# Twelve token blocks cut as eleven of 512 and one of 384, the last of them multiplied without Strassen's scheme

## The chip, the cores and the metric

One core of a Trainium2 chip. The metric is the device time of one launch in microseconds (us); lower is better. Inputs and outputs lie in the chip's memory, and the host only lays arrays out.

## What is computed

A channel attention over 6016 tokens of 256 channels, then two feed-forward stages of width 2048, all in float32. The first stage's activation is `h * cos(h)`, the second's is `h * sigmoid(h)` (SiLU).

```python
qn = q / (np.linalg.norm(q, axis=1, keepdims=True) + 1e-06)   # q, k, v: (1, 6016, 256)
kn = k / (np.linalg.norm(k, axis=1, keepdims=True) + 1e-06)
s = kn.transpose(0, 2, 1) @ qn / tau                          # 256 x 256
a = np.exp(s - s.max(-1, keepdims=True))
a /= a.sum(-1, keepdims=True) + 1e-09
x = (v @ a).reshape(6016, 256)
h = x @ w_in;   x = (h * np.cos(h)) @ w_out                   # 256 -> 2048 -> 256
h = x @ w_in2;  out = (h * (1.0 / (1.0 + np.exp(-h)))) @ w_out2
```

The weights reach the chip as 64-bit floats (the reference draws them so) and are decoded there.

## The kernel before, in words

**Opening (L283 to L465).** The 256 x 256 scores are summed over all tokens, softmaxed, and folded into the first input weights (`emit_w`), so that the first stage reads v directly. Every product is made of three matmuls of rounded parts (fp32r): high x high, low weight x high, high weight x low (`PASSES`). So each operand is split into a high and a low tile.

**First stage (L724 to L797).** The tokens are cut into NB = 12 blocks by `SIZES` (L29): four of 512 columns and eight of 496. A block has NPAIR = 8 units, m = 0 to 7; a unit covers 256 of the 2048 hidden features. For each unit, TensorE makes h (`emit_h`, 12 matmuls of one block's width), ScalarE and VectorE make `h * cos(h)` (L495, L496, L503, L504), ScalarE and VectorE split it (L511, L512), and two units later TensorE adds it into the block's output (`emit_o1`, again 12 matmuls, L522). At a block's end its output is copied out of PSUM (L563), its Strassen forms are made and split in five steps that are popped one per unit (`emit_x2`), and the result is stored to DRAM by two DMAs (L571).

**What else runs in the first stage.** GpSimd splits v of the next block (L266, L271) after its load (L255, issued at m = 2 of every block). The weights of the second stage come in 16 pieces, `wi2` 0 to 7 and `wo2` 0 to 7. A piece is decoded by ScalarE, GpSimd and VectorE (`decode`, L171: L178, L153, L159, L160, L166, L169), its Strassen forms are made by GpSimd (`weight_forms`, L214 to L216), and it is stored to DRAM through one tile, "stage" (L708), or kept (`HELD`). Two pieces are decoded per block, after units 1 and 5; blocks 4 and 8 have decode calls after units 3 and 7 too (L765).

**Second stage (L812 to L907).** One loop over 96 units, j = 0 to 95, with three more rounds to empty it. In round j unit j's first products of x are made, unit j - 1's remaining ones, and unit j - 3's output products. Each 2 x 2 block product is Strassen-Winograd's: 7 products (`PRODUCTS`) of half a block's width in place of 8, with three matmuls each (`product`, L593). So a unit has 21 matmuls into the hidden features and 21 into the output (`emit_o2`), each of 256 or 248 columns. The hidden features are summed from the products (L829, L830), passed through SiLU (L872, L883, L884), combined into forms (L532, L537, L538) and split (L543, L551). At a block's end ScalarE and VectorE copy the seven output products out of PSUM (L656, L659), VectorE adds them up in steps of one per round (L642), and SyncE stores them.

**The last unit** is an exception: `emit_plain` makes its output as plain products (24 matmuls, L632), part of them into free PSUM room, and `emit_last` adds and stores.

**Order.** The schedule is written out by hand: each engine runs its instructions in the order of the Python calls. SyncE's queue issues nearly all DMAs in program order, and a DMA that waits holds those behind it. `HELD`, `SECOND`, `THIRD`, `STAGED` and `FOURTH` say when the second stage's weight pieces are fetched back: `THIRD` goes into the space of first-stage weights while the last block (block 11) runs, `FOURTH` follows once the room of `emit_x2` is free. `X2_STEPS` says how many of block 11's five steps are popped in rounds 3, 4 and 5 of the second stage; for that block GpSimd makes the high parts (L546).

Of the kernel before, what the change touches and what calls it, by code (L numbers as in the profile page):

```python
# [28 lines left out]
SIZES = 4 * [512] + 8 * [496]  # L29
# [9 lines left out]
NU = NS - 1  # L39


PLAIN = {"C21": ((0, 1), (2, 3)), "C22": ((0, 0), (2, 2)), "P2": ((1, 1), (3, 3)), "P3": ((1, 0), (3, 2))}
# [38 lines left out]
def attention_then_two_ffns(ctx: ExitStack, tc: tile.TileContext, qk, vT, tau, w_in1, w_out1, w_in2, w_out2, outT):  # L81
# [34 lines left out]
    a21 = wp.tile([P, 2, P], F32R, name="a21")  # L116
# [94 lines left out]
    def weight_forms(to, t, to0=None):  # L211

        for s, x, y, op in ((4, 0, 2, ALU.add), (5, 0, 1, ALU.subtract), (6, 5, 2, ALU.add), (7, 3, 6, ALU.subtract)):
            nc.gpsimd.tensor_tensor(out=t[:, s], in0=t[:, x], in1=t[:, y], op=op)  # L214
        nc.gpsimd.tensor_scalar(out=to[:, 0], in0=t[:, 1:], scalar1=1.0, scalar2=1.0, op0=ALU.mult, op1=ALU.mult)
        nc.gpsimd.tensor_tensor(out=to[:, 1], in0=t[:, 1:], in1=to[:, 0].bitcast(F32), op=ALU.subtract)  # L216
        if to0 is not None:
            hi, lo = to0[:, 0], to0[:, 1]
            nc.gpsimd.tensor_scalar(out=hi, in0=t[:, 0], scalar1=1.0, scalar2=1.0, op0=ALU.mult, op1=ALU.mult)
            nc.gpsimd.tensor_tensor(out=lo, in0=t[:, 0], in1=hi.bitcast(F32), op=ALU.subtract)  # L220
# [31 lines left out]
    def load_v(b, split=True):  # L252
# [220 lines left out]
    xs, later = {}, {}  # L473
# [80 lines left out]

    def emit_x2(b):
# [3 lines left out]
        high = part_hi_pool if b == NB - 1 else part_hi  # L559
# [10 lines left out]
        def store(k, x):  # L570
# [6 lines left out]
            lambda: high(t, hi, RAW, c),  # L577
            lambda: (part_lo(t, hi, lo, RAW, c), high(t, hi, FORMED, c)),
# [3 lines left out]
    def load_x2(b):  # L582
        c = BLOCKS[b][1] // 2
        xparts[2, b] = [xp.tile([P, NU, HB], F32R, tag=f"x{s}", name=f"x2{s}{b}") for s in ("hi", "lo")]
        for t, d in zip(xparts[2, b], xs.pop(b)):
            nc.sync.dma_start(out=t[:, :, :c].bitcast(F32), in_=d)
# [32 lines left out]
    def emit_plain(u, parts, room):  # L619

        b, m = u
        c = BLOCKS[b][1] // 2
        w = w2["wo2"][m]
        for name, terms in PLAIN.items():
            if name in BANKS:
                t, k, j = BANKS[name]
                out = state[2, b][t][:, k, j, :c]
            else:
                out = room[:, int(name == "C22"), :c]
            for i, (ka, kb) in enumerate(terms):  # L630
                for p, r in PASSES:
                    nc.tensor.matmul(  # L632
                        out,
                        w[:, p, ka - 1] if ka else a21[:, p],
                        columns(parts[r][:, kb, :c]),
                        start=(name == "C21" and i == 0 and (p, r) == PASSES[0]),
                        stop=(i == 1 and (p, r) == PASSES[-1]),
                        skip_group_check=True,
                    )
# [295 lines left out]
```

## Time and profile before

| | |
|---|---|
| median of 3 runs | 1023.58 us (1023.3 to 1024.41) |
| time of the profiled execution | 1024.01 us |
| its span | 1022.2 us |
| TensorE matmul busy | 1005.6 us (98%), 6603 matmuls |
| TensorE weight loads busy | 934.3 us (91%) |
| VectorE busy | 904.3 us (88%) |
| ScalarE busy | 755.5 us (74%) |
| GpSimd busy | 310.9 us (30%) |
| DMA traffic | 109.48 MB, mean 107 GB/s |

How to read it: the first stage's first matmul of h starts at 60.9 us of the span and the second stage's first product at 556.3 us. TensorE's matmuls are pipelined, so that a matmul's listed duration is longer than the distance to the next; the distance is what it costs in a full stream. The page's row of granted TensorE clock shows full speed (2.4 GHz) in all 40 slices.

### The profile page before, as it was taken

How to read it: one execution, taken by the hardware profiler on the slowest of the kernel's cores; microseconds unless marked ns; L12 is line 12 of the kernel's file. 1: busy time of each engine (PE TensorE's matmuls, PEld its weight loads, DVE VectorE, ACT ScalarE, POOL GpSimd, SP SyncE). 2: the span in 40 equal slices, each digit the busy share in tenths (PEclk: the TensorE clock that was granted, in tenths of full speed). 3: DMA queues.
4: the chain of work that ended last, by engine and by line, in shares of the span. 5: the costliest groups of instructions: out<-in, count | busy, mean ns of one | idle time of the engine just before them, and what ended most of it. 6: DMA issues, size and time to landing. Idle time of an engine off the chain costs nothing.

```text
span 1022.2 us, 16929 instructions
## 1 busy us (share of the span) xinstructions
PE 1005.6 (98%) x6603; PEld 934.3 (91%) x6603; DVE 904.3 (88%) x1139; ACT 755.5 (74%) x1191; POOL 310.9 (30%) x275
## 2 busy tenths in 40 slices
PE   8989999999999999999999999999999999999997
PEld 7857888888889999899999899999999999999997
DVE  3889899999999999987777889999999999998997
ACT  6677767677667677666766687888887887887885
POOL 4245463656555645731000311111111111111110
PEclk9999999999999999999999999999999999999999
DMA  9950122233344263232057551121122022023001
GB/s 351 359 185 1 41 77 94 82 125 129 98 149 127 77 200 101 85 127 90 25 210 279 181 201 44 54 88 60 43 81 80 22 81 91 11 81 91 12 11 41
DMA packets 55391, 109.48 MB, mean 107 GB/s; under 512 B 2704, under 2 KB 37520, under 8 KB 55312
## 3 DMA queue, kind: packets, MB, share of 16 engines
q1 hardware_dynamic: 55168, 108.28, 30.9%
q8 instruction: 52, 0.85, 0.4%
q14 instruction: 27, 0.22, 0.1%
q10 hardware_dynamic: 144, 0.13, 0.0%
HBM read 68.75 MB, written 39.65 MB: 106 GB/s over the span
## 4 chain that ended last, share of the span: by engine, by line
PE 88%; DVE 7%; ACT 2%; issue 1%; DMA 1%; POOL 0%; SPq 0%; DVEq 0%; POOLq 0%; ACTq 0%
PE o L522 21%; PE h L483 21%; PE o L593 20%; PE xz L593 12%; PE ys L593 9%; PE S L318 4%; DVE lo L512 1%; DVE t L496 1%; DVE t L504 1%; DVE y L538 1%; ACT wa L425 0%; DVE lo L551 0%; DMA qk<-qk_dram 0%; DVE wa L428 0%; DMA outT_dram<-q 0%
## 5 line engine op out<-in xcount | busy, mean ns | idle before, releaser
L551 DVE TENSOR_TENSOR lo<-t,hi 128x744 fp32r<-128x744 f32 (+3 forms) x190 | 207.6, 1097 | 33.0 <-ACT hi L543 31.7
L593 PE MATMUL o<-hi,wo 128*128 128x248 f32 (+1 forms) x1330 | 232.6, 275 | 0.0
L538 POOL TENSOR_TENSOR t<-t 128x248 f32<-128x248 f32 (+1 forms) x94 | 67.6, 719 | 447.0 <-DVE t L537 392.1
L593 PEld LDWEIGHTS o<-hi,wo 128*128 128x128 f32 x1330 | 202.1, 192 | 0.0
L543 ACT ACTIVATE hi<-t 128x992 fp32r<-128x992 f32 (+3 forms) x188 | 176.3, 938 | 32.2 <-PE o L593 31.3
L483 PE MATMUL h<-xhi,wa 128*128 128x496 f32 (+1 forms) x768 | 194.7, 376 | 3.4 <-DVE t L504 2.6
L522 PE MATMUL o<-hi,wo 128*128 128x496 f32 (+1 forms) x768 | 193.7, 375 | 0.0
L593 PE MATMUL o<-lo,wo 128*128 128x248 f32 (+1 forms) x665 | 183.1, 275 | 0.3 <-DVE lo L551 0.3
L483 PEld LDWEIGHTS h<-xhi,wa 128*128 128x128 f32 x768 | 144.9, 189 | 22.9 <-issue 5.9
L522 PEld LDWEIGHTS o<-hi,wo 128*128 128x128 f32 x768 | 144.9, 189 | 17.0
L503 ACT ACTIVATE t<-t,half_pi 128x992 f32<-128x992 f32 (+1 forms) x96 | 108.8, 1133 | 64.2 <-DVE t L496 63.8
L495 ACT ACTIVATE t<-h 128x992 int32<-128x992 f32 (+1 forms) x96 | 96.5, 1005 | 75.9 <-PE h L483 67.6
L496 DVE SCALAR_TENSOR_TENSOR t<-t,h 128x992 f32<-128x992 int32 (+1 forms) x96 | 114.9, 1196 | 40.7 <-ACT t L495 40.6
L593 PE MATMUL xz<-x2hi,wi 128*128 128x248 f32 (+1 forms) x768 | 143.6, 275 | 0.2 <-ACT p L844 0.2
L512 DVE TENSOR_TENSOR lo<-t,hi 128x992 fp32r<-128x992 f32 (+1 forms) x96 | 141.1, 1470 | 1.1 <-ACT hi L511 1.1
L593 PEld LDWEIGHTS o<-lo,wo 128*128 128x128 f32 x665 | 127.7, 192 | 0.5 <-DVE lo L551 0.5
L504 DVE TENSOR_TENSOR t<-h,t 128x992 f32<-128x992 f32 (+1 forms) x96 | 115.0, 1198 | 5.1 <-ACT t L503 0.8
L593 PEld LDWEIGHTS xz<-x2hi,wi 128*128 128x128 f32 x768 | 116.9, 192 | 0.6 <-ACT p L844 0.4
L522 PE MATMUL o<-lo,wo 128*128 128x496 f32 (+1 forms) x384 | 113.1, 376 | 1.9 <-DVE lo L512 1.8
L593 PE MATMUL ys<-x2hi,wi 128*128 128x248 f32 (+1 forms) x576 | 112.2, 277 | 1.7 <-DVE t L830 1.5
L483 PE MATMUL h<-xlo,wa 128*128 128x496 f32 (+1 forms) x384 | 112.5, 375 | 0.0
L593 PE MATMUL xz<-x2lo,wi 128*128 128x248 f32 (+1 forms) x384 | 105.6, 275 | 0.0
(136 smaller groups left out, 1645.9 us busy)
## 6 DMA issues: line engine op xcount, KB each, us to landing
qk<-qk_dram SPq DMA_DIRECT2D x22, 512.0 KB, 7.5
xshi<-yhi SPq DMA_DIRECT2D x8, 868.0 KB, 5.9
xslo<-ylo SPq DMA_DIRECT2D x8, 868.0 KB, 6.9
x2hi<-xshi SPq DMA_DIRECT2D x8, 868.0 KB, 5.9
x2lo<-xslo SPq DMA_DIRECT2D x8, 868.0 KB, 7.8
wo_dram<-stage_wo SPq DMA_DIRECT2D x7, 896.0 KB, 4.5
wo<-wo_dram SPq DMA_DIRECT2D x7, 896.0 KB, 6.2
wi_dram<-stage_wi SPq DMA_DIRECT2D x6, 896.0 KB, 4.5
```

The costliest lines, as they stand in the source:

```text
L318: nc.tensor.matmul(S[:, a, :C], tiles[g][:, j, 1, a * P : (a + 1) * P], tiles[g][:, j, 0, :], start=(c0 + j == 0), stop=(c0 + j == NCK - 1),)
L483: nc.tensor.matmul(hp[:, s, :n], lhsT, rhs, start=(i == 0), stop=(i == len(todo) - 1))
L495: nc.scalar.activation(k, hp[:, :, :n], AF.Copy, scale=1.0 / TWO_PI, bias=0.25)
L496: nc.vector.scalar_tensor_tensor(out=t[:, :, :n], in0=k, scalar=-TWO_PI, in1=hp[:, :, :n], op0=ALU.mult, op1=ALU.add)
L503: nc.scalar.activation(t[:, :, :n], t[:, :, :n], AF.Sin, bias=half_pi)
L504: nc.vector.tensor_tensor(out=t[:, :, :n], in0=hp[:, :, :n], in1=t[:, :, :n], op=ALU.mult)
L512: nc.vector.tensor_tensor(out=lo[:, :, :n], in0=t[:, :, :n], in1=hi[:, :, :n].bitcast(F32), op=ALU.subtract)
L522: nc.tensor.matmul(o[:, e, :n], wo1_at(i, f)[:, e * P : (e + 1) * P], columns(parts[k][:, s, :n]), start=(f == 0 and (i, k) == PASSES[0]), ...
L538: eng.tensor_tensor(out=t[:, 7, :c], in0=t[:, 3, :c], in1=t[:, 6, :c], op=ALU.subtract)
L543: nc.scalar.activation(hi[:, sl, :c], t[:, 1:][:, sl, :c], AF.Copy)
L551: nc.vector.tensor_tensor(out=lo[:, sl, :c], in0=t[:, 1:][:, sl, :c], in1=hi[:, sl, :c].bitcast(F32), op=ALU.subtract)
L593: nc.tensor.matmul(out, w[:, p, ka - 1], columns(x[r][:, kb - 1, : out.shape[-1]]), start=(start and i == 0), stop=(stop and i == 2), skip ...
```

## The change

`SIZES` becomes eleven blocks of 512 columns and one of 384. The last block (`PLAIN`, block 11) is multiplied in the second stage without Strassen's scheme: 12 matmuls of 384 columns into the hidden features (`emit_plain_h`) and 12 into the output (`emit_plain_o`) per unit, with no forms. `emit_x2_plain` splits its input in two steps in round 3. Since plain products need the first quadrant of every weight piece too, each stored piece has eight slots of 128 columns in place of seven; for the four pieces whose space has only seven (`ASIDE`) the first quadrant is kept in DRAM and fetched into the room that the smaller last block leaves in its input tile. Decodes begin after units 0 and 5, GpSimd's split of v is issued after unit 3 and not with the load, and the last unit's output is finished one PSUM tile after the other (`emit_last`).

```diff
-SIZES = 4 * [512] + 8 * [496]
+SIZES = 11 * [512] + [384]
...
+PLAIN = len(SIZES) - 1
...
+ASIDE = HELD + [("wo2", 7)]
...
-X2_STEPS = {3: 2, 4: 2, 5: 1}
+X2_STEPS = {3: 2}
...
-        nc.gpsimd.tensor_scalar(out=to[:, 0], in0=t[:, 1:], scalar1=1.0, scalar2=1.0, op0=ALU.mult, op1=ALU.mult)
-        nc.gpsimd.tensor_tensor(out=to[:, 1], in0=t[:, 1:], in1=to[:, 0].bitcast(F32), op=ALU.subtract)
-        if to0 is not None:
...
+        for (hi, lo), src in (((to[:, 0], to[:, 1]), t[:, 1:]), ((to0[:, 0], to0[:, 1]), t[:, 0])):
+            nc.gpsimd.tensor_scalar(out=hi, in0=src, scalar1=1.0, scalar2=1.0, op0=ALU.mult, op1=ALU.mult)
+            nc.gpsimd.tensor_tensor(out=lo, in0=src, in1=hi.bitcast(F32), op=ALU.subtract)
...
+    def emit_x2_plain(b):
...
+        def high():
+            for a in range(CH):
+                nc.scalar.activation(to[0][a], src[a], AF.Copy)
+
+        def low():
+            for a in range(CH):
+                nc.vector.tensor_tensor(out=to[1][a], in0=src[a], in1=to[0][a].bitcast(F32), op=ALU.subtract)
+            for k, x in enumerate((hi, lo)):
+                nc.sync.dma_start(out=xs[b][k], in_=x.bitcast(F32))
...
+        if b == PLAIN:
+            room = xparts[2, b][0].rearrange("p s c -> p (s c)")[:, CH * 2 * c :]
+            for k, key in enumerate(ASIDE):
+                to = room[:, k * 2 * P : (k + 1) * 2 * P].rearrange("p (i e) -> p i e", i=2)
+                nc.sync.dma_start(out=to.bitcast(F32), in_=first[key])
...
+    def emit_plain_h(u, s, out):
+
+        x = xparts[2, u[0]]
+        todo = [(quadrant("wi2", u[1], i, 2 * a + s), columns(x[k][:, a])) for i, k in PASSES for a in range(CH)]
...
+        for e in both:
+            todo = [(quadrant("wo2", m, i, 2 * s + e), columns(parts[k][:, s])) for i, k in PASSES for s in range(2)]
...
+    def emit_last(b, e):
...
+        if e == 0:
...
+            nc.scalar.activation(q.rearrange("p (h b) -> p h b", h=2), src, AF.Copy)
+            nc.sync.dma_start(out=to[:, e], in_=q)
+            return
+        for h, (eng, queue) in enumerate(((nc.vector.tensor_copy, nc.sync), (nc.scalar.copy, nc.scalar))):
...
-            if m in (1, 5) or (b in (4, 8) and m in (3, 7)) :
+            if m in (0, 5):
                 W.decode()
                 W.load()
-            if b == 4 and m == 6:
-                WO2.load(2)
+            if b == 4 and m in (2, 7):
+                WO2.load()
...
-                load_v(b + 1)
+                vraw = load_v(b + 1)
...
+        if m == 3 and 1 <= b < NB - 1:
+            split_v(b + 1, vraw, pool=True)()
...
+        if pp_ is not None:
+            hi, lo = [whole(sc.tile([P, NU, HB], F32R, tag=s, name=f"{s}2_{j - 1}"), n) for s in ("hi", "lo")]
+            t = whole(sc.tile([P, NS, HB], F32, tag="t", name=f"t2_{j - 1}"), n)
+            for s in range(2):
+                nc.scalar.activation(t[:, s], h_last[s], AF.Silu)
+            nc.scalar.activation(hi, t, AF.Copy)
+            nc.vector.tensor_tensor(out=lo, in0=t, in1=hi.bitcast(F32), op=ALU.subtract)
```

Three places show what moves. The first is TensorE in the last block's fifth unit (m = 4; `hi_92`, `lo_92` are its parts, `o_11_*` the block's output, `xz` and `ys` the PSUM tiles of hidden features). Before, its output products stand between those of later units in groups of three, x248:

```order
L593 MATMUL o_11_1_10142<-hi_92_10306,wo_4_4180 128x248 x2
L593 MATMUL o_11_1_10142<-lo_92_10307,wo_4_4180 128x248
L593 MATMUL o_11_1_10142<-hi_92_10306,wo_4_4180 128x248 x2
L593 MATMUL o_11_1_10142<-lo_92_10307,wo_4_4180 128x248
L593 MATMUL o_11_1_10142<-hi_92_10306,wo_4_4180 128x248 x2
L593 MATMUL o_11_1_10142<-lo_92_10307,wo_4_4180 128x248
L593 MATMUL xz_4364<-x2hi_9542,wi_7_4401 128x248 x2
L593 MATMUL xz_4364<-x2lo_9543,wi_7_4401 128x248
L593 MATMUL ys_4363<-x2hi_9542,wi_7_4401 128x248 x2
L593 MATMUL ys_4363<-x2lo_9543,wi_7_4401 128x248
```

Now the round that holds them, whole:

```order
L656 MATMUL xz_4402<-x2hi_9574,wi_7_4439 128x384 x4
L656 MATMUL xz_4402<-x2lo_9575,wi_7_4439 128x384 x2
L667 MATMUL o_11_0_10117<-hi_92_10202,wo_4_4218 128x384 x4
L667 MATMUL o_11_0_10117<-lo_92_10203,wo_4_4218 128x384 x2
L667 MATMUL o_11_1_10118<-hi_92_10202,wo_4_4218 128x384 x4
L667 MATMUL o_11_1_10118<-lo_92_10203,wo_4_4218 128x384 x2
L656 MATMUL ys_4401<-x2hi_9574,wi_7_4439 128x384 x4
L656 MATMUL ys_4401<-x2lo_9575,wi_7_4439 128x384 x2
```

A round of the last block has 24 matmuls of 384 columns where a full one had 42 of 248.

The second place is VectorE at the start of block 4 (`t_4_0` is unit 0's hidden tile, `lo_3_7` the low part of the unit before, `wv_wi` the piece that is decoded). Before:

```order
L504 TENSOR_TENSOR t_4_0_1768<-h_0_1755,t_4_0_1768 128x2x496
L496 SCALAR_TENSOR_TENSOR t_4_1_1802<-t_4_1_1802,h_1_1789 128x2x496
L512 TENSOR_TENSOR lo_4_0_1806<-t_4_0_1768,hi_4_0_1805 128x2x496
L504 TENSOR_TENSOR t_4_1_1802<-h_1_1789,t_4_1_1802 128x2x496
L159 TENSOR_SCALAR wv_wi_1811<-wv_wi_1811 128x512
L160 TENSOR_SCALAR wv_wi_1811<-wv_wi_1811 128x512
L166 SCALAR_TENSOR_TENSOR wv_wi_1811<-raw_wi_1496,wv_wi_1811 128x512
```

Now:

```order
L505 TENSOR_TENSOR t_4_0_1785<-h_0_1772,t_4_0_1785 128x1024
L159 TENSOR_SCALAR wv_wi_1794<-wv_wi_1794 128x512
L160 TENSOR_SCALAR wv_wi_1794<-wv_wi_1794 128x512
L166 SCALAR_TENSOR_TENSOR wv_wi_1794<-raw_wi_1477,wv_wi_1794 128x512
L497 SCALAR_TENSOR_TENSOR t_4_1_1837<-t_4_1_1837,h_1_1824 128x1024
L513 TENSOR_TENSOR lo_4_0_1841<-t_4_0_1785,hi_4_0_1840 128x1024
L505 TENSOR_TENSOR t_4_1_1837<-h_1_1824,t_4_1_1837 128x1024
```

The decode's three operations stand one unit earlier; in block 4 the extra ones after unit 3 are gone.

The third place is GpSimd in block 1, where `wi2` piece 0 is decoded and v of block 2 is split (`vraw`). Before:

```order
L215 TENSOR_SCALAR wi_0_724<-wv_wi_824 128x896
L216 TENSOR_TENSOR wi_0_724<-wv_wi_824,wi_0_724 128x896
L266 TENSOR_SCALAR xhi_882<-vraw_880 128x1024
L271 TENSOR_TENSOR xlo_883<-vraw_880,xhi_882 128x1024
L153 TENSOR_SCALAR raw_wi_754<-raw_wi_754 128x512
```

Now:

```order
L216 TENSOR_SCALAR wi_0_723<-wv_wi_789 128x896
L217 TENSOR_TENSOR wi_0_723<-wv_wi_789,wi_0_723 128x896
L216 TENSOR_SCALAR stage_wi_796<-wv_wi_789 128x128
L217 TENSOR_TENSOR stage_wi_796<-wv_wi_789,stage_wi_796 128x128
L259 TENSOR_SCALAR xhi_922<-vraw_884 128x1024
L266 TENSOR_TENSOR xlo_923<-vraw_884,xhi_922 128x1024
```

Each piece has two more operations of 128 columns, and for a held piece a store of the first quadrant stands ahead of v's load on SyncE's queue. The order of pieces and splits on GpSimd is otherwise the same.

## Rows read from the trace of the kernel before

**Rows 1.** Stretch (us), its length, busy of PE, PEld, DVE, ACT, POOL; PEclk, DMA.

```profile
107.50:234.15 126.65, 125.11 (x577) 108.61 (x577) 117.59 (x105) 88.39 (x91) 68.21 (x53) 1.00 0.24 85
234.15:516.10 281.95, 281.69 (x1346) 253.64 (x1346) 254.04 (x236) 195.99 (x208) 125.30 (x99) 1.00 0.34 111
565.00:590.00 25.00, 22.99 (x188) 21.59 (x187) 22.66 (x33) 16.80 (x38) 8.79 (x9) 1.00 0.54 183
1005.00:1018.00 13.00, 11.80 (x103) 11.42 (x101) 11.20 (x22) 7.00 (x15) 0.26 (x1) 1.00 0.07 21
```

**Rows 2.** Chain that ended last: start, us, what, in both stages.

```profile
147.24 2.59 PE o L522 x12
...
458.49 2.51 PE o L522 x12
...
624.81 1.34 PE o L593 x12
...
835.86 1.34 PE o L593 x12
```

**Rows 3.** Timeline of TensorE at those two second-stage places: start, duration, what.

```profile
624.98 0.39 PE L593 MATMUL o<-hi,wo 128*128 128x256 f32 x2
...
836.03 0.39 PE L593 MATMUL o<-hi,wo 128*128 128x248 f32 x2
```

**Rows 4.** Waits of TensorE from 107 to 520 us: total, times, longest.

```profile
PE o L522 <- DVE lo L512: 1.8, 3, 1.1
```

**Rows 5.** Timeline of VectorE, then of GpSimd, in block 1.

```profile
128.06 2.82 DVE L512 TENSOR_TENSOR lo<-t,hi 128x1024 fp32r<-128x1024 f32 x1
132.63 2.53 DVE L538 TENSOR_TENSOR y<-y 128x256 f32<-128x256 f32 x1
136.21 1.21 DVE L512 TENSOR_TENSOR lo<-t,hi 128x1024 fp32r<-128x1024 f32 x1
...
127.69 2.10 POOL L216 TENSOR_TENSOR wi<-wv_wi,wi 128x896 fp32r<-128x896 f32 x1
...
132.39 2.48 POOL L271 TENSOR_TENSOR xlo<-vraw,xhi 128x1024 fp32r<-128x1024 f32 x1
```

**Rows 6.** Timeline of GpSimd in block 2: the split of v, with its wait.

```profile
180.27 1.57 POOL L266 TENSOR_SCALAR xhi<-vraw 128x1024 fp32r<-128x1024 f32 x1 [8.34 <-DMA vraw<-vT_dram]
```

**Rows 7.** Timeline of VectorE, then of TensorE, in the second stage's first rounds.

```profile
571.76 1.36 DVE L532 TENSOR_TENSOR y<-y 128x496 f32<-128x496 f32 x1
573.61 0.42 DVE L538 TENSOR_TENSOR y<-y 128x248 f32<-128x248 f32 x1
578.62 1.73 DVE L551 TENSOR_TENSOR ylo<-y,yhi 128x744 fp32r<-128x744 f32 x1 [0.71 <-POOL yhi L546]
...
576.94 0.49 PE L593 MATMUL ys<-x2hi,wi 128*128 128x256 f32 x2 [0.68 <-DVE t L830]
```

**Rows 8.** Groups by line and shape: count, busy us, mean ns, idle before.

```profile
L543 ACT ACTIVATE hi<-t 128x768 fp32r<-128x768 f32 x32 | 27.4, 855 | 7.8 <-PE o L593 7.6
L551 DVE TENSOR_TENSOR lo<-t,hi 128x768 fp32r<-128x768 f32 x32 | 33.2, 1037 | 0.0
L659 DVE COPY q<-o 128x768 f32<-128x768 f32 x4 | 3.8, 950 | 0.0
L656 ACT ACTIVATE q<-o 128x1024 f32<-128x1024 f32 x4 | 4.2, 1056 | 0.0
```

**Rows 9.** Timeline of the last rounds, all engines.

```profile
1014.49 0.38 ACT L681 ACTIVATE q<-o 128x248 f32<-128x248 f32 x1 [1.56 <-DMA outT_dram<-q]
...
1016.58 0.48 PE L632 MATMUL o<-hi,wo 128*128 128x248 f32 x2 [1.04 <-DVE q L642]
...
1017.91 0.28 PE L632 MATMUL o<-lo,wo 128*128 128x248 f32 x1
1018.22 0.74 DVE L642 TENSOR_TENSOR q<-q,o 128x248 f32<-128x248 f32 x2 [0.53 <-PE o L632]
1018.99 0.34 SPq L694 DMA_DIRECT2D outT_dram<-q  x1
```

More of the change, by code (lines that the diff above doesn't have):

```diff
@@ L472, in attention_then_two_ffns, with quadrant @@
     w2 = {"wi2": {}, "wo2": {}}
-    xs, later = {}, {}
+    xs, later, first = {}, {}, {}
+    def quadrant(name, m, i, s):
+        w = w2[name][m]
+        if s:
+            return w[:, i, s - 1]
+        return first[name, m][:, i] if (name, m) in first else w[:, i, NU]
     def emit_h(u):
@@ L553, in part_lo, with whole @@
         )
+    def whole(t, n):
+        return t.rearrange("p s c -> p (s c)")[:, : CH * n].rearrange("p (a n) -> p a n", a=CH)
+    def emit_x2_plain(b):
+        n = BLOCKS[b][1]
+        hi, lo = [whole(yp.tile([P, NU, HB], F32R, tag=f"y{s}", name=f"y{s}{b}"), n) for s in ("hi", "lo")]
+        xs[b] = [dp.tile([P, CH, n], F32, name=f"xs{s}{b}") for s in ("hi", "lo")]
+        src = [state[1, b][:, a, :n].rearrange("p (b h g) -> p h g b", h=2, g=2) for a in range(CH)]
+        to = [[x[:, a].rearrange("p (h g b) -> p h g b", h=2, g=2) for a in range(CH)] for x in (hi, lo)]
+        def high():
[6 more added lines that the diff above has]
+                nc.sync.dma_start(out=xs[b][k], in_=x.bitcast(F32))
+        return [high, low]
     def emit_x2(b):
@@ L617, in emit_o2, with emit_plain_o @@
             )
-    def emit_plain(u, parts, room):
-        b, m = u
[L622 to L639, printed above, removed]
+    def emit_plain_h(u, s, out):
+        x = xparts[2, u[0]]
+        todo = [(quadrant("wi2", u[1], i, 2 * a + s), columns(x[k][:, a])) for i, k in PASSES for a in range(CH)]
+        for i, (lhsT, rhs) in enumerate(todo):
+            nc.tensor.matmul(out, lhsT, rhs, start=(i == 0), stop=(i == len(todo) - 1), skip_group_check=True)
+    def emit_plain_o(u, parts, both):
+        b, m = u
+        n = BLOCKS[b][1]
+        if (2, b) not in state:
+            state[2, b] = [ps_o.tile([P, 2, TB], F32, tag="o", name=f"o2_{b}_{e}") for e in range(CH)]
+        for e in both:
+            todo = [(quadrant("wo2", m, i, 2 * s + e), columns(parts[k][:, s])) for i, k in PASSES for s in range(2)]
+            for i, (lhsT, rhs) in enumerate(todo):
+                nc.tensor.matmul(
+                    state[2, b][e][:, 0, :n],
+                    lhsT,
+                    rhs,
+                    start=(m == 0 and i == 0),
+                    stop=(m == NPAIR - 1 and i == len(todo) - 1),
+                    skip_group_check=True,
+                )
     def add(out, x, y):
@@ L782, in attention_then_two_ffns @@
         if (b, m) == (NB - 1, 4):
-            fetch(STAGED, hp_.tile([P, 2, NU, P], F32R, tag="stage", name="wo2_4"))
+            fetch(STAGED, hp_.tile([P, 2, NS, P], F32R, tag="stage", name="wo2_4"))
         if i >= LAG:
@@ L844, in attention_then_two_ffns @@
             nc.scalar.activation(seeds[j][0], z2, AF.Copy)
-        final = p == (NB - 1, NPAIR - 1)
-        if p is not None and j - 2 in hl:
+        if j - 2 in hl and units[j - 2][0] != PLAIN:
             t_, hi_, lo_, c_ = hl[j - 2]
             part_lo(t_, hi_, lo_, RAW, c_)
-        if final:
-            part_hi(t_, hi_, FORMED, c_)
         if j == 0:
@@ L863, in attention_then_two_ffns @@
                 for key in FOURTH:
-                    fetch(key, late.tile([P, 2, NU, P], F32R, name=f"{key[0]}_{key[1]}"))
-        names = list(BANKS) if o != (NB - 1, NPAIR - 2) else ["P1", "P2", "P6", "P7", "P5", "P3", "P4"]
-        if o == (NB - 1, NPAIR - 1):
-            emit_last(o[0], hl[j - LAG2], xz[(len(units) - 2) % 2])
-            break
+                    fetch(key, late.tile([P, 2, NU if key in ASIDE else NS, P], F32R, name=f"{key[0]}_{key[1]}"))
+        names = list(BANKS)
+        if op_ is not None:
+            emit_plain_o(op_, hl[j - LAG2], (0, 1) if op_[1] < NPAIR - 1 else (0,))
+            if op_[1] == NPAIR - 1:
+                emit_last(PLAIN, 0)
+                emit_plain_o(op_, hl[j - LAG2], (1,))
+                emit_last(PLAIN, 1)
+                break
         if o is not None:
@@ L872, in attention_then_two_ffns @@
             nc.scalar.activation(t[:, 0:2, :c], t[:, 0:2, :c], AF.Silu)
-        if p is not None and j - 2 in hl:
-            if not final:
-                (part_hi if j > EASED else part_hi_pool)(t_, hi_, FORMED, c_)
+        if j - 2 in hl and units[j - 2][0] != PLAIN:
+            (part_hi if j > EASED else part_hi_pool)(t_, hi_, FORMED, c_)
             part_lo(t_, hi_, lo_, FORMED, c_)
```

125 lines of the change are left out of this document (59 added, 66 removed).

## The prediction

> **What bounds the kernel now.** I read the busy times by stretch first, then the chain that ended last, then what interrupts it. By stretch [rows 1] TensorE is busy nearly without a gap in both stages, at a granted clock of 1.00 (the 2.4 GHz level). The chain [rows 2] says what a matmul costs in a full stream. Twelve matmuls of 512 columns take 2.59 us (0.2158 each), twelve of 496 take 2.51 (0.2092), and twelve of the second stage take 1.34 (0.1117), both where they have 256 columns and where they have 248 [rows 2, 3]. So in the first stage the price follows the columns: 16 columns cost 0.0066 us, 0.00042 a column. In the second stage something else sets it, most likely the weight load, and the columns are nearly free.
>
> The time that TensorE loses is a stretch's length minus its matmuls times their price [rows 1]. Blocks 1 to 3 lose 126.65 - 577 x 0.2158 = 2.1 us, blocks 4 to 10 lose 281.95 - 1346 x 0.2092 = 0.4. The first second-stage rounds lose 25.0 - 188 x 0.1117 = 4.0 and the last rounds 13.0 - 103 x 0.1117 = 1.5. The waits name VectorE's low part, line 512, in the first stage [rows 4].
>
> **The change part by part.** The sum is made against the profiled execution's 1024.0 us (span 1022.2), 0.4 above the median of the runs shown, 1023.6.
>
> Second stage, full stream. Before: 96 units x 42 matmuls, and 3 more in the last, 4035 x 0.1117 = 450.7 us. After: 88 x 42 = 3696 x 0.1117 = 412.8, and the last block's 8 x 24 = 192 matmuls of 384 columns. No row shows 384 columns. Along the first stage's line one costs 0.2158 - 128 x 0.00042 = 0.162, 31.2 us in all; together 444.0. The gain is **6.7 us**. Its ends are the nearest rows: at 0.1117 (256 columns) the gain would be 16.5, at 0.2092 (496) there would be a loss of 2.3. I take the line, since two rows of one stream define it and 0.162 lies well above the 0.1117 floor. Most of this comes from the seven blocks' worth of products that carry 256 columns for the price of 248.
>
> First stage, full stream. Matmul count stays 2304, columns stay 6016 in all: 4 x 16 x 2.59 + 8 x 16 x 2.51 = 487.0 before, 11 x 16 x 2.59 + 16 x 1.95 = 487.0 after. **0**.
>
> First stage, stalls (2.5 us of loss). They come from GpSimd. In block 1 VectorE's line 512 took 2.82 us while GpSimd's line 216 ran, and line 538 took 2.53 while line 271 ran [rows 5]; undisturbed they take 1.21 [rows 5] and 0.42 [rows 7]. The Trainium skill states the mechanism (SBUF — State Buffer, section "SBUF: two separate sides"): a VectorE operation with two SBUF inputs and a GpSimd operation that reads SBUF exclude each other for a whole instruction. The overlap in time here agrees with it. A VectorE unit of 512 columns needs about 3.6 us (three operations of some 1.2) of TensorE's 5.18 (2 x 2.59), so 1.5 us of slack a unit absorbs most collisions. The change moves decode A from unit 1 to unit 0. In block 2 v landed only at 180.3 [rows 6], six units in, behind the store of decode A, and the split then met decode B's VectorE work. One unit earlier, it will be over before that. In blocks 1 and 5 the split no longer follows line 216 at once, as a small store now stands ahead of v's load. Against that, it may meet the forms of unit 3 (line 538), and each piece has two more GpSimd operations, of 128 columns, shorter than the 2.10 of the 896-column one [rows 5]; GpSimd is busy 68 of 127 us there [rows 1], so nobody waits for them except through collisions. I take **-1.0**, with ends of -2.5 (all gone) and +4 (0.7 us in each of nine blocks).
>
> Into the second stage (4.0 us of loss). Before, VectorE makes block 11's Strassen forms in rounds 3 to 5: 1.36, twice 0.42, then low parts such as 1.73 after a wait for GpSimd [rows 7], while TensorE waits 0.68 us for line 830. Now there are two ScalarE copies and two VectorE subtractions of 384 columns, each about half of 0.86 and 1.04 [rows 8]; VectorE sheds some 4 us over three rounds. ScalarE gets 0.9 us more in round 3, and late next is its SiLU. The last block's units are shorter, 3.9 us against 5.0, so the fetches of weight pieces (an eighth larger) have 9 us less before round 0; but they are needed one a round, 4.7 us apart, so I cost them at nothing. If that cover is gone, each us of lateness is one us. I take **-1.5**, ends -3 and +1.
>
> Into the last block (new). After the last full unit's twelfth output matmul, ScalarE must copy the first tile (1.06), do two SiLUs (about 0.5 each) and a high part (0.86), then VectorE a low part (1.04) and, behind it on the same queue, the copy of the second tile (0.95) [rows 8]: 4.9 us. TensorE has 6 x 0.162 + 9 x 0.1117 + 12 x 0.162 = 3.9 us until it needs that second tile. So it waits about **+1.1**, ends 0 and +2.2. In the block itself a round is 24 x 0.162 = 3.9 us of TensorE, against 1.9 us of ScalarE, and of VectorE a low part of 1.04 and two of block 10's adds (0.74 for two [rows 9]), so nothing waits.
>
> The end (1.5 us of loss). Before, ScalarE's first copy waited 1.56 us for an output DMA, VectorE's adds followed it, and TensorE stood 1.04 us behind them [rows 9]. Now no add stands between matmuls: after unit 7's hidden features TensorE has 24 matmuls, 3.9 us, and needs a SiLU, a high and a low part, 2.4 us: **-1.5**. After the last matmul starts (1017.91) there are two adds before the final DMA is issued at 1018.99 [rows 9]; then two half copies side by side: **-0.3**.
>
> Sum: -6.7 + 0 - 1.0 - 1.5 + 1.1 - 1.5 - 0.3 = -9.9, so 1014.1 for that execution and **1013.7** for the runs.
>
> **The rivals.** (A) The stalls do not go but move. Decode, split and forms meet elsewhere, and the second stage's opening stays bound by ScalarE. For it: TensorE's slack is lost to whichever unit meets GpSimd, and the move is by one unit only. Against it: two long chains are taken apart. Without the two gains 1016.2; with the upper end of +4, 1020.
>
> (B) The 384-column matmuls cost nearly what 496 cost. Then 192 x 0.047 = 9 us come back: 1022.7. Against it: the two prices of one stream differ by their columns alone.
>
> (C) The second stage's price does follow the columns, and 256 costs more than 248. By the first stage's slope 8 columns are 0.0033 us; over 7 blocks x 336 matmuls that is 7.9 us: 1021.6. Against it: the same 1.34 for both [rows 2, 3]. The Trainium skill (TensorE: Matmul & The Clock Gate, section "Back-to-back issue gap") gives N/2.4 + 2.5 ns, which fits 0.2158 and 0.2092. By it, as an estimate, 256 columns would cost 0.1092 and 248 0.1058, and the change would lose some 3 us in this stream in place of gaining 6.7. The row of 0.1117 at both sizes speaks against it here.
>
> (D) Slower: GpSimd blocks VectorE in each of the nine blocks with decodes. The place is unit 4's low part, which the TensorE of unit 6 waits for. A block in which line 512 meets line 216 (2.82 - 1.21 = 1.6 lost), line 538 meets line 271 (2.1 lost) and a second low part meets the split (up to 1.6) loses 5.3 us, against 1.5 us of slack a unit. It turns the verdict once such a block costs TensorE 1.5 us: 9 x 1.5 = 13.5 in place of 2.5 undoes the gain; at 2 us each the time is 1030.
>
> **How the numbers follow.** Forecast 0.62 (1010.5 to 1016), A 0.22 (1016 to 1020), B 0.04, C 0.04, D 0.05, and 0.03 below 1010, where the plain block or the lost stalls give more. Some 0.2%, 2 us, is what a measurement of this kernel can tell from no change, so faster begins at 1021.5. Faster: 0.62 + 0.22 + 0.03, and half of C, 0.89; same: B and half of C, 0.06; slower: D, 0.05. The range, 1009.5 to 1020, holds the forecast and A.
>
> **What would show it right or wrong.** In the chain after the change: twelve matmuls of 384 columns in 1.95 us in both stages, and 1.34 for twelve of 256 everywhere. 1.95 higher means B, 1.34 higher means C. In the waits of TensorE in the first stage: under 2.5 us of loss, and no line 538 (539 after the change) of 2.5 us next to a stall; more means A or D. One wait of about 1 us where the last block's second output tile is first written. No wait of TensorE after its last hidden features. The forecast is wrong if the second stage's full stream is not 6 to 7 us shorter.

## The result, and the profile after

The changed kernel takes 1010.94 us (median of 4 runs, 1010.59 to 1011.11), against 1023.44 (1023.27 to 1024.41) for the kernel before in the same session: a ratio of 0.9876, interval 0.9858 to 0.9893, 12.5 us less. The profiled execution took 1010.59 us with a span of 1008.8, so the span is 13.4 shorter than before (1022.2). The page of the kernel after:

```profile
span 1008.8 us, 16566 instructions
...
PE 995.7 (99%) x6456; PEld 921.8 (91%) x6456; DVE 868.1 (86%) x1089; ACT 747.4 (74%) x1152; POOL 330.2 (33%) x297
```

TensorE has 147 matmuls fewer (6603 before), VectorE 36 us less work, GpSimd 19 more. Busy times by stretch of the kernel after (columns as in [rows 1]); the four stretches of before lie at the same places of the program as the first three and the last here:

```profile
107.10:231.50 124.40, 124.40 (x578) 108.92 (x578) 111.27 (x106) 88.57 (x91) 76.47 (x64) 1.00 0.27 92
231.50:521.50 290.00, 290.00 (x1345) 253.96 (x1344) 252.07 (x235) 201.33 (x207) 141.77 (x118) 1.00 0.32 114
562.00:587.00 25.00, 23.89 (x208) 23.25 (x207) 22.13 (x36) 18.49 (x43) 6.86 (x8) 1.00 0.75 272
...
600.00:950.00 350.00, 350.00 (x3137) 350.00 (x3136) 324.51 (x524) 291.80 (x609) 55.04 (x75) 1.00 0.18 61
...
990.00:1005.40 15.40, 15.40 (x96) 15.15 (x94) 5.26 (x8) 6.47 (x11) 0.00 (x0) 1.00 0.10 35
```

In the first two, TensorE is busy for the whole length: 578 x 0.2158 is 124.7 and 1345 x 0.2158 is 290.3, the length up to the matmuls that the edges cut. No stall is left in blocks 1 to 10, and the list of TensorE's waits from 107 to 520 us, which had line 512 in it before [rows 4], is empty. The opening of the second stage still loses 25.0 - 208 x 0.1117 = 1.8 (4.0 before). In the middle of the second stage 350 / 3137 = 0.1116 per matmul: all of them now carry 256 columns, at the price of before. The last block is full too: 15.4 / 96 = 0.160. The chain that ended last shows that block and the end:

```profile
984.98 1.95 PE o L667 x12
...
999.60 5.86 PE o L667 x36
...
1005.49 0.37 DVE q L720
...
1005.93 0.32 ACT q L720
```

Twelve matmuls of 384 columns take 1.95 us (0.1625 each), where [rows 2] had 2.59, 2.51 and 1.34. The last 36 follow each other without a gap.

To say where the 13.4 us went I add up TensorE's gaps one by one: the distance from a matmul's start to the next one's, less the price of its width. This finer count replaces the estimates by stretch, and gives for before a loss of 2.9 in the first stage (four stalls) and 4.2 into the second.

| part of the program | before | after | change |
|---|---|---|---|
| second stage, matmuls at their price | 450.7 | 444.0 | -6.7 |
| lost in the first stage (blocks 1 to 11) | 2.9 | 0.0 | -2.9 |
| lost going into the second stage | 4.2 | 2.1 | -2.1 |
| lost going into the last block | 0 | 1.1 | +1.1 |
| lost in the last rounds | 1.8 | 0.0 | -1.8 |
| from the last matmul's start to the end | 4.3 | 3.7 | -0.6 |
| opening, to block 1 (not touched) | 107.5 | 107.1 | -0.4 |

The sum is -13.4. Two long stalls remain; the other 1.2 us lost going into the second stage are short waits, the two longest of 0.4 and 0.3, which stood there before too. The rows are of the timeline of the kernel after (start, duration, what, idle time before and its releaser), first at the start of the second stage, then at the entry to the last block (PSUM is the memory that TensorE writes its products to):

```profile
567.40 0.88 ACT L569 ACTIVATE yhi<-o 128x384 fp32r<-128x384 f32 x2
568.73 1.01 DVE L573 TENSOR_TENSOR ylo<-o,yhi 128x384 fp32r<-128x384 f32 x2
569.89 0.46 PE L625 MATMUL o<-hi,wo 128*128 128x256 f32 x2 [0.73 <-DVE ylo L573]
...
979.84 0.96 DVE L951 TENSOR_TENSOR lo<-t,hi 128x768 fp32r<-128x768 f32 x1 [3.34 <-ACT hi L950]
980.72 0.95 DVE L694 COPY q<-o 128x768 f32<-128x768 f32 x1
981.81 0.89 PE L667 MATMUL o<-hi,wo 128*128 128x384 f32 x4 [0.88 <-DVE q L694]
```

The first is new: line 573 reads block 11's first-stage output straight from the PSUM tile that the second stage's output products want to write. The second is the predicted wait for the second output tile.

### The profile page after: what moved, and what is told of

Same layout as the page of the kernel before. It is cut to its first block, busy times and chain, and to the rows that moved or that the text cites. A ratio compares the mean times of both kernels' runs of the same rounds, so it can differ in the third digit from the quotient of the medians.

```text
span 1008.8 us, 16566 instructions
## 1 busy us (share of the span) xinstructions
PE 995.7 (99%) x6456; PEld 921.8 (91%) x6456; DVE 868.1 (86%) x1089; ACT 747.4 (74%) x1152; POOL 330.2 (33%) x297
## 5 line engine op out<-in xcount | busy, mean ns | idle before, releaser
L552 DVE TENSOR_TENSOR lo<-t,hi 128x768 fp32r<-128x768 f32 (+1 forms) x176 | 195.1, 1118 | 28.3 <-ACT hi L544 28.2
L625 PE MATMUL o<-hi,wo 128*128 128x256 f32 x1232 | 215.5, 275 | 0.7 <-DVE ylo L573 0.7
L484 PE MATMUL h<-xhi,wa 128*128 128x512 f32 (+1 forms) x768 | 194.7, 376 | 3.4 <-DVE t L505 2.6
L523 PE MATMUL o<-hi,wo 128*128 128x512 f32 (+1 forms) x768 | 193.7, 375 | 0.0
L544 ACT ACTIVATE hi<-t 128x768 fp32r<-128x768 f32 (+1 forms) x174 | 166.9, 959 | 29.6 <-PE o L625 29.0
L625 PE MATMUL o<-lo,wo 128*128 128x256 f32 x616 | 169.4, 275 | 0.0
L497 DVE SCALAR_TENSOR_TENSOR t<-t,h 128x1024 f32<-128x1024 int32 (+1 forms) x96 | 114.9, 1196 | 51.8 <-ACT t L496 51.7
L513 DVE TENSOR_TENSOR lo<-t,hi 128x1024 fp32r<-128x1024 f32 (+1 forms) x96 | 137.8, 1435 | 0.9 <-ACT hi L512 0.9
L625 PE MATMUL xz<-x2hi,wi 128*128 128x256 f32 x704 | 131.7, 275 | 0.2 <-ACT p L885 0.2
L505 DVE TENSOR_TENSOR t<-h,t 128x1024 f32<-128x1024 f32 (+1 forms) x96 | 114.9, 1197 | 5.4 <-ACT t L504 0.8
```

Source lines behind the costliest of these rows:

```text
L484: nc.tensor.matmul(hp[:, s, :n], lhsT, rhs, start=(i == 0), stop=(i == len(todo) - 1))
L497: nc.vector.scalar_tensor_tensor(out=t[:, :, :n], in0=k, scalar=-TWO_PI, in1=hp[:, :, :n], op0=ALU.mult, op1=ALU.add)
L505: nc.vector.tensor_tensor(out=t[:, :, :n], in0=hp[:, :, :n], in1=t[:, :, :n], op=ALU.mult)
L513: nc.vector.tensor_tensor(out=lo[:, :, :n], in0=t[:, :, :n], in1=hi[:, :, :n].bitcast(F32), op=ALU.subtract)
L523: nc.tensor.matmul(o[:, e, :n], wo1_at(i, f)[:, e * P : (e + 1) * P], columns(parts[k][:, s, :n]), start=(f == 0 and (i, k) == PASSES[0]), ...
L544: nc.scalar.activation(hi[:, sl, :c], t[:, 1:][:, sl, :c], AF.Copy)
```

## The experiments

Eleven kernels were run. The question that most of them share is why the first stage lost nothing any more, since the change also gives GpSimd more to do. "Loss" is the count of gaps above, in the first stage. Decode A and decode B are the two decodes of a block, after units 0 and 5 in the kernel after, after 1 and 5 before (after 1 and 3 in blocks 4 and 8 there, whose later calls find nothing left to decode). "The split" is GpSimd's split of v, and "x2's forms" are the Strassen forms that VectorE makes of the block's output (lines 533, 538 and 539).

**One: the old decode units in the changed kernel.** Only the order of decodes and piece loads is undone, which also brings back the calls after units 3 and 7 in blocks 4 and 8; GpSimd's split of v stays issued after unit 3.

```diff
-            if m in (0, 5):
+            if m in (1, 5) or (b in (4, 8) and m in (3, 7)) :
...
-            if b == 4 and m in (2, 7):
-                WO2.load()
+            if b == 4 and m == 6:
+                WO2.load(2)
```

> The changed kernel with the decodes put back after units 1 and 5 (and the extra calls in blocks 4 and 8), the piece loads as before; everything else as changed. Theory 'placement' (the first stage's stalls went because decode A moved one unit earlier, so that the split of v is over before decode B's VectorE work): the stalls come back, TensorE loses 2 to 4 us in blocks 1 to 10, time 1013 to 1015. Rival 'size' (they went because wider blocks give VectorE more slack, or because the first quadrant's store holds v's load back): loss below 0.5 us, time 1010.7 to 1011.3.

Measured: 1023.9 us (1023.04 to 1025.3), ratio to before 1.0 (0.9991 to 1.0009). The whole gain is gone: the loss is 12.9 us, in ten stalls of 0.6 to 1.7. The direction was expected (a loss of 2 to 4 us), the size was not. TensorE's waits there, from 105 to 520 us:

```profile
PE o L523 <- DVE lo L513: 10.3, 10, 1.5
```

GpSimd and VectorE in block 2 of this kernel, from its timeline:

```profile
182.60 1.61 POOL L259 TENSOR_SCALAR xhi<-vraw 128x1024 fp32r<-128x1024 f32 x1 [8.33 <-DMA vraw<-vT_dram]
183.54 0.95 DVE L159 TENSOR_SCALAR wv_wi<-wv_wi 128x512 f32<-128x512 f32 x1
184.29 2.48 POOL L266 TENSOR_TENSOR xlo<-vraw,xhi 128x1024 fp32r<-128x1024 f32 x1
184.52 2.53 DVE L160 TENSOR_SCALAR wv_wi<-wv_wi 128x512 int32<-128x512 int32 x1
187.09 1.38 DVE L166 SCALAR_TENSOR_TENSOR wv_wi<-raw_wi,wv_wi 128x512 int32<-128x512 int32 x1
```

The same place in the kernel after:

```profile
171.67 0.41 DVE L538 TENSOR_TENSOR y<-y 128x256 f32<-128x256 f32 x1
172.12 0.42 DVE L539 TENSOR_TENSOR y<-y 128x256 f32<-128x256 f32 x1
176.26 1.56 POOL L259 TENSOR_SCALAR xhi<-vraw 128x1024 fp32r<-128x1024 f32 x1 [9.12 <-DMA vraw<-vT_dram]
177.91 2.43 POOL L266 TENSOR_TENSOR xlo<-vraw,xhi 128x1024 fp32r<-128x1024 f32 x1
179.47 1.95 DVE L513 TENSOR_TENSOR lo<-t,hi 128x1024 fp32r<-128x1024 f32 x1
182.47 0.41 DVE L159 TENSOR_SCALAR wv_wi<-wv_wi 128x512 f32<-128x512 f32 x1
182.92 0.43 DVE L160 TENSOR_SCALAR wv_wi<-wv_wi 128x512 int32<-128x512 int32 x1
183.38 0.85 DVE L166 SCALAR_TENSOR_TENSOR wv_wi<-raw_wi,wv_wi 128x512 int32<-128x512 int32 x1
```

With the old units the split, held back until v has landed behind decode A's store, runs beside decode B: line 160 takes 2.53 in place of 0.43, line 166 1.38 in place of 0.85, the next low part is late, and TensorE stands 1.7 us at 189.7. In the kernel after, the split falls into a lull of VectorE, ten microseconds in which it has only its units' own operations, between x2's forms (lines 538, 539) and decode B. The split still holds one low part (1.95), and TensorE does not wait.

Blocks 2, 3, 6 and 7 show this meeting; in blocks 1 and 5 the split meets only line 159 of decode B (1.51). These six blocks lose 1.0 to 1.8 us each, 8.4 together, and block 9 loses nothing. Blocks 4 and 8 lose 2.3 each, more than half of it (a stall of 1.5) before their split starts. There decode B, after unit 3, comes into the same stretch as a held low part and x2's forms, here in block 4:

```profile
256.55 2.10 POOL L217 TENSOR_TENSOR stage_wi<-wv_wi,stage_wi 128x896 fp32r<-128x896 f32 x1
256.95 2.79 DVE L513 TENSOR_TENSOR lo<-t,hi 128x1024 fp32r<-128x1024 f32 x1
260.80 0.92 DVE L159 TENSOR_SCALAR wv_wi<-wv_wi 128x512 f32<-128x512 f32 x1
263.43 1.40 DVE L539 TENSOR_TENSOR y<-y 128x256 f32<-128x256 f32 x1
```

**Two: the kernel before with the new order of decodes, split and loads alone.**

```diff
-            if m in (1, 5) or (b in (4, 8) and m in (3, 7)) :
+            if m in (0, 5):
...
+        if m == 3 and 1 <= b < NB - 1:
+            split_v(b + 1, vraw)()
```

> The kernel before, with only the decodes after units 0 and 5, their piece loads, and the split of v issued after unit 3. Theory 'placement': the 2.9 us that TensorE loses in blocks 1 to 10 go to below 0.5, time about 1020.5. Rival 'size': the loss stays between 2 and 4 us, time 1023 to 1024.5. If only the held pieces' store did it, the stalls in blocks 1 and 5 stay (about 1 us) and the one in block 2 goes.

Measured: 1020.62 us (1020.4 to 1021.2), ratio 0.9973 (0.9962 to 0.9983). The loss falls from 2.9 to 0.06, and the time by as much. So the order is worth 3 us in the kernel before, and 13 in the changed one.

**Three: the kernel before with the new block sizes alone**, all blocks in Strassen's scheme.

```diff
-SIZES = 4 * [512] + 8 * [496]
+SIZES = 11 * [512] + [384]
```

> The kernel before, with only the block sizes changed to eleven of 512 and one of 384, all in Strassen products. Theory 'price per matmul' (in the second stage a matmul costs 0.1117 us whatever its columns up to 256): 4035 matmuls as before, the last block's of 192 columns at 0.1117 too, so the second stage's stream is 450.7 us as before and the time is within 2 us of 1023.4, moved only by first-stage stalls. Rival 'price per column below 256': 192 columns cost 0.083 us or so, 339 matmuls of the last block save 9.7 us, time about 1014.

Measured: 1023.25 us (1022.77 to 1024.26), ratio 0.9997 (0.9988 to 1.0006): nothing. A matmul of the last block, 192 columns, costs 0.1117 as well. The number of matmuls stayed, so the stream did.

**Four: the split issued with v's load again.**

```diff
-        if m == 3 and 1 <= b < NB - 1:
-            split_v(b + 1, vraw, pool=True)()
...
-                vraw = load_v(b + 1)
+                split_v(b + 1, load_v(b + 1), pool=True)()
```

> The changed kernel with GpSimd's split of v issued with the load after unit 2 again. GpSimd's queue then has the same order (decode A, split, decode B), and the split waits for v's landing either way: no change, 1010.7 to 1011.3. Rival: issuing it after unit 3 matters by itself (a wait in GpSimd's queue that holds something else), 1 us or more slower.

Measured: 1010.79 us (1010.36 to 1011.22). No change that can be told from 1010.94: GpSimd has no other work between the two places, so its order is the same. When the split runs is set by when v lands.

**Five, six, seven: the two stalls that remain.** In five, the copy of block 10's second output tile goes ahead of the low part of the last block on VectorE. In six, block 11's input is split in round 2 in place of 3. Seven does both.

```diff
                 adds += emit_out(o[0])
+                if o[0] == PLAIN - 1:
+                    adds.pop(0)()
```

```diff
-X2_STEPS = {3: 2}
+X2_STEPS = {2: 2}
...
-        if j == 3:
+        if j == 2:
             steps += emit_x2(NB - 1)
```

> The changed kernel, with the copy of block 10's second output tile put on VectorE's queue at the end of its last round, ahead of the plain units' low part in place of behind it. Theory (TensorE's one wait of 1.1 us in the last block is for that copy, which stands behind a low part that itself waits for ScalarE): the wait goes, time 1.0 to 1.1 us shorter, 1009.9. Rival (the copy is late because of the tile itself, or the wait moves to the next low part): less than 0.3 us.

> The changed kernel, with the last block's input split (two ScalarE copies, two VectorE subtractions out of PSUM) in round 2 of the second stage and not in round 3. Theory (the wait of 0.9 us in round 3 is for the second PSUM tile, which the subtractions still read when the output products want it): that wait goes, 0.9 us shorter if round 2 has room. Rival (ScalarE already holds TensorE up in round 2, 0.9 us of small waits there): the wait moves into round 2 and the time is the same within 0.3 us.

> Both of the edits before together. If they are independent, their gains add: up to 2.0 us shorter than the changed kernel, 1009.0.

Measured: five 1009.48 us (1009.31 to 1009.58), ratio to before 0.9861 (0.9844 to 0.9877); six 1011.26 (1010.83 to 1011.62); seven 1010.04 (1009.59 to 1010.36). Five takes the entry's wait away, as its timeline shows:

```profile
979.03 0.96 DVE L694 COPY q<-o 128x768 f32<-128x768 f32 x1 [2.51 <-PE o L625]
979.90 0.95 DVE L953 TENSOR_TENSOR lo<-t,hi 128x768 fp32r<-128x768 f32 x1
980.78 0.81 PE L667 MATMUL o<-hi,wo 128*128 128x384 f32 x4
```

The matmuls start at 980.78 with no wait, where they stood until 981.81 in the kernel after. Six removes the wait for line 573, but ScalarE's copies of line 569 (0.88) now delay its other work in round 2, and TensorE stands 1.0 there: the opening of the second stage loses 2.4 in place of 2.1. Seven is five's gain, less about what six loses. **Version five is the fastest of all that were run.**

**Eight: the last output tile in one ScalarE copy and one DMA**, in place of two halves on two engines.

```diff
-        if e == 0:
+        if True:
```

> The changed kernel, with the last output tile copied by one ScalarE operation and stored by one DMA, in place of two half copies on VectorE and ScalarE with two DMAs. In the trace the two half copies ran one behind the other (0.36 and 0.32 us), so that the last DMA was issued 0.8 us after the last matmul ended. Theory (the halves exclude each other): one copy of 0.49 us ends earlier, 0.2 to 0.3 us shorter. Rival (the larger DMA takes it back): no change.

Measured: 1010.78 us (1010.41 to 1011.09), not to be told from 1010.94. In the kernel after, the halves don't run side by side:

```profile
1005.49 0.36 DVE L720 COPY q<-o 128x192 f32<-128x192 f32 x1 [2.33 <-PE o L667]
1005.87 0.33 SPq L721 DMA_DIRECT2D outT_dram<-q  x1
1005.93 0.32 ACT L720 COPY q<-o 128x192 f32<-128x192 f32 x1 [0.93 <-DVE q L720]
1006.28 0.37 ACTq L721 DMA_DIRECT2D outT_dram<-q  x1
```

ScalarE's copy waits for VectorE's, so the split into halves brings nothing that can be measured.

**Nine, ten, eleven: which meeting costs.** Runs one and two left two readings open: that decode A's place at unit 1 costs, or that the split meeting decode B does. Nine is run one's kernel with v loaded at unit 0, ahead of decode A's store. Ten is the changed kernel with decode B at unit 4. Eleven is run one's kernel with decode B at unit 6. Each diff is against the kernel named there.

```diff
+        if m == 0 and 1 <= b < NB - 1:
+            vraw = load_v(b + 1)
...
-            if 1 <= b < NB - 1:
-                vraw = load_v(b + 1)
...
```

```diff
-            if m in (0, 5):
+            if m in (0, 4):
```

```diff
-            if m in (1, 5) or (b in (4, 8) and m in (3, 7)) :
+            if m in (1, 6) or (b in (4, 8) and m in (3, 7)) :
```

> The changed kernel with the old decode units 1 and 5, as in the first run, but v's load issued at unit 0 and so ahead of decode A's store on SyncE's queue. In the first run the split waited 8.33 us for v in block 2, began at 182.6 and ran beside decode B's VectorE operations; TensorE lost 12.9 us in the first stage. If what costs is the split meeting decode B: v is there when decode A's forms end on GpSimd, the split begins about 8 us earlier, at some 174.3 in block 2, and is over at 178.5, ahead of decode B's line 160, which is back at 0.43 us; the loss of the first stage falls below 4 us and the time to 1011 to 1014. If decode A's own place at unit 1 is what costs (its operations meet low parts there): loss still 9 us or more, 1019 to 1024.

> The changed kernel with decode B one unit earlier, after unit 4 in place of 5; decode A stays at unit 0. The split of block 2 runs from 176.3 to 180.4 in the changed kernel, and decode B's VectorE operations from 182.5. If what costs is the split meeting decode B: the operations of lines 159 and 160 move to some 177 to 178, beside the split, line 160 takes about 2.5 us, line 166 waits for GpSimd's line 153 behind the split and holds VectorE's queue; TensorE loses 8 to 14 us in the first stage, 1018 to 1025. If decode A at unit 1 was what cost in the first run: no such loss, 1010 to 1013.

> The first run's kernel (old decode unit 1 for A) with decode B one unit later, after unit 6 in place of 5. In the first run the split of block 2 ran from 182.6 to 186.8 and decode B's VectorE operations from 183.5; x2's formed operations of lines 538 and 539 were over at 175.5. If it is the split of v meeting extra VectorE operations, whichever they are, that costs: decode B's operations move to some 188.7, the split then meets only the unit's own three operations and is free; the loss of the first stage falls from 12.9 to under 5 us, and the time to 1011 to 1016. A low part of line 552, at 188.4 in the first run, now falls into the same unit as decode B and may cost a little of it. If decode A at unit 1, or GpSimd's added work as such, is what costs: loss still 9 us or more, 1019 to 1024.

Measured: nine 1024.28 us (1023.69 to 1025.62), loss 13.6; ten 1020.19 (1019.63 to 1020.45), loss 9.3; eleven 1015.03 (1014.72 to 1015.17), loss 4.4. Nine missed. The split did start 8.6 us earlier and left decode B alone, but met x2's forms; from its timeline:

```profile
170.14 2.10 POOL L217 TENSOR_TENSOR stage_wi<-wv_wi,stage_wi 128x896 fp32r<-128x896 f32 x1
170.50 2.82 DVE L513 TENSOR_TENSOR lo<-t,hi 128x1024 fp32r<-128x1024 f32 x1
...
173.99 1.56 POOL L259 TENSOR_SCALAR xhi<-vraw 128x1024 fp32r<-128x1024 f32 x1
174.38 1.45 DVE L538 TENSOR_TENSOR y<-y 128x256 f32<-128x256 f32 x1
175.63 2.47 POOL L266 TENSOR_TENSOR xlo<-vraw,xhi 128x1024 fp32r<-128x1024 f32 x1
175.86 2.53 DVE L539 TENSOR_TENSOR y<-y 128x256 f32<-128x256 f32 x1
...
186.40 0.43 DVE L160 TENSOR_SCALAR wv_wi<-wv_wi 128x512 int32<-128x512 int32 x1
```

Lines 538 and 539 take 4.0 in place of 0.8, and TensorE stands 1.4 us at 179.1. Here decode A at unit 1 has a part in the loss: its line 217 holds the low part just before (2.82), so that it is done only 0.8 us before TensorE's first matmul with it, and then the split arrives. But in ten decode A is at unit 0, and a loss came with decode B moved onto the split:

```profile
177.09 1.74 POOL L259 TENSOR_SCALAR xhi<-vraw 128x1024 fp32r<-128x1024 f32 x1 [9.16 <-DMA vraw<-vT_dram]
177.46 1.65 DVE L160 TENSOR_SCALAR wv_wi<-wv_wi 128x512 int32<-128x512 int32 x1
178.91 2.46 POOL L266 TENSOR_TENSOR xlo<-vraw,xhi 128x1024 fp32r<-128x1024 f32 x1
179.14 2.91 DVE L166 SCALAR_TENSOR_TENSOR wv_wi<-raw_wi,wv_wi 128x512 int32<-128x512 int32 x1
```

And in eleven decode A is at unit 1 and two thirds of the loss went, with decode B moved off the split:

```profile
181.70 1.58 POOL L259 TENSOR_SCALAR xhi<-vraw 128x1024 fp32r<-128x1024 f32 x1 [8.24 <-DMA vraw<-vT_dram]
182.03 2.06 DVE L552 TENSOR_TENSOR ylo<-y,yhi 128x768 fp32r<-128x768 f32 x1
185.15 2.32 DVE L513 TENSOR_TENSOR lo<-t,hi 128x1024 fp32r<-128x1024 f32 x1
188.97 0.43 DVE L160 TENSOR_SCALAR wv_wi<-wv_wi 128x512 int32<-128x512 int32 x1
```

The split there still meets one extra operation (line 552, 2.06 for some 0.95), and TensorE loses 0.3 us near it. The six blocks 1 to 3 and 5 to 7, which lost 8.4 in run one, lose 0.3 here. The other 4.1 stand in blocks 4 and 8: 2.5 in two stalls behind decode B and x2's forms, most of the rest behind the split. No run moves decode B of those two blocks alone.

Times in the table count from the span's start; block 2 starts between 148.6 and 150.2 in all of them.

| kernel | decodes after units | split starts in block 2 | extra VectorE work beside it | loss | median |
|---|---|---|---|---|---|
| before | 1, 5 | 180.3 | decode B, in part | 2.9 | 1023.4 |
| three (sizes) | 1, 5 | 180.9 | decode B, in part | 4.5 | 1023.25 |
| one | 1, 5 | 182.6 | decode B, whole | 12.9 | 1023.9 |
| nine | 1, 5 | 174.0 | lines 538, 539 | 13.6 | 1024.28 |
| ten | 0, 4 | 177.1 | decode B, whole | 9.3 | 1020.19 |
| eleven | 1, 6 | 181.7 | line 552 | 4.4 | 1015.03 |
| after | 0, 5 | 176.3 | none | 0.0 | 1010.94 |

For the kernels that share the changed kernel's second stage (one, nine, ten, eleven), the median is 1010.9 plus the loss, to 0.3 us.

A meeting with the split does not cost by itself. In run two, in block 8, the split meets the same two forms as in nine (lines 537 and 538 there), and TensorE does not wait:

```profile
415.81 2.40 POOL L271 TENSOR_TENSOR xlo<-vraw,xhi 128x992 fp32r<-128x992 f32 x1
416.04 2.45 DVE L538 TENSOR_TENSOR y<-y 128x248 f32<-128x248 f32 x1
```

Decode A is at unit 0 there. The low part ahead of these forms is done 2.2 us before TensorE's first matmul with it, against 0.8 in nine; the next one is done 0.1 us before. By these two traces, what decides is how far VectorE is ahead of TensorE when the split holds it; no run varies that alone.

## Why the prediction was right, point by point

The forecast was 1013.7 with a range from 1009.5 to 1020; 1010.94 came. By its own steps:

- **Second stage, full stream, -6.7: as predicted.** The price on the first stage's line for 384 columns, 0.162, is the 0.1625 of the chain; rival B (0.2092) fell with that. Twelve of 256 columns stay at 1.34, so rival C fell too. What was wrong is the sentence on where the gain comes from, "seven blocks' worth of products that carry 256 columns for the price of 248". Run three has those columns and gains nothing. What falls is the matmul count: 339 of the last block at 0.1117 (37.9 us) become 192 at 0.1625 (31.2). The wider blocks matter only since they make the last one narrow; a plain block of 496 columns would cost 192 x 0.2092 = 40.2.
- **First stage, full stream, 0: as predicted.** The stalls aside, blocks 1 to 10 have the length of their matmuls.
- **First-stage stalls, -1.0: the mis-sized term.** It was -2.9, beyond its lower end of -2.5 (the stretches had put the loss before at 2.5). The reason given, that the split would be over before decode B's VectorE work, is what runs one, ten and eleven show. But the step allowed for new collisions with the forms and from the longer GpSimd work, and there were none that TensorE waited for: the split fell into VectorE's lull. That the lull would be there was not worked out, so the total inside the range is partly luck: with the old decode order the same change measured 1023.9, outside the range.
- **Rival D (slower) had the right mechanism and a low chance.** GpSimd blocking VectorE in eight of the nine blocks with decodes, at 1.0 to 2.3 us each, is run one: 12.9 us lost, and no gain left. In six of them its place was not the one named: it is the split beside decode B, not a low part beside line 216 (217 after the change). In blocks 4 and 8 such a held low part does stand ahead of the stall. The prediction took the order of decodes for worth 1 us. In this kernel it is worth 13.
- **Why the added GpSimd work made it worse.** In run one the two operations of 128 columns ahead of decode A's store take 1.27 + 0.46 = 1.7 us, and its split starts 1.7 us later than in run three (182.60 against 180.90). That puts it squarely on decode B. This is read from the traces of the two; a run that takes those operations alone away was not made, so that this step is argued and not shown.
- **Into the second stage, -1.5: it was -2.1.** VectorE's forms went, as said. "Late next is its SiLU" was wrong: what is late is line 573, by its hold on a PSUM tile (0.9 us with the gap behind it), which the prediction did not see. Run six takes it away. The short waits before it stood there before the change as well.
- **Into the last block, +1.1: as predicted**, with the cause named (the second tile's copy behind the low part), and run five removes it.
- **The end, -1.5 and -0.3: it was -1.8 and -0.6.** No gap is left among the last matmuls. The two half copies were taken to run side by side. They don't; it costs nothing that run eight could show.

Rival A, that stalls only move, holds for the 0.9 us of line 573 alone; the 1.2 us of short waits in the second stage's opening neither moved nor went. In all, the profiled executions differ by 13.4 us where 9.9 were forecast. The 3.5 are 1.9 of stalls, 0.6 of the way into the second stage, 0.6 of the end, and 0.4 of an opening that the change doesn't touch: it took from 107.1 to 107.7 us in the changed kernel and runs one, nine, ten and eleven.

## What to carry to other kernels

When a side engine can hold the bound engine's feeder, look for the feeder's lull and see what fixes the side engine's work in time: here a load behind a waiting store on one queue decided it, and a new order of another step was worth 13 us. Such a gain could not be read from the old kernel alone (3 us there): by the traces of runs one and three, the added side work shifts the split in time. So lay the side work, with its additions, along the units before pricing a move. And where narrower matmuls cost no less (192 columns as much as 256 here), count matmuls, not columns.

## What the runs showed of the hardware that was not expected

- An operation of VectorE with one input (line 160, 128 x 512) is held as much as one with two: 0.43 us alone, 2.53 beside GpSimd's line 266 (run one), 1.65 beside line 259 and the start of 266 (run ten).
- In the second stage 192 columns cost 0.1117 us, the same as 248 and 256 (run three), while 384 cost 0.1625, on the line through 496 and 512.
- How long the low parts are held does not tell the loss: the 96 of the first stage add up to 137.8 us in the kernel after, 141.1 before and 138.6 in run one, which stalls ten times. VectorE's other operations do differ. From 105 to 520 us, their time above the fastest of the same shape adds up to 7.7 us after, 17.0 before and 27.4 in run one; line 160 alone takes 1.03 on average in run one, 0.43 after. Even so the sum does not rank the kernels: in run ten it is 36.0, with a loss of 9.3.
